# Two reorderings on ScalarE in a fused convolution, gate and projection kernel

## The chip, the cores and the metric

The kernel runs on one core of one Trainium2 chip. The metric is the device time of one execution in microseconds (us); lower is better. Three runs of the kernel before gave 386.8 to 387.71, with a median of 387.55.

A core has five engines with a queue each: TensorE (PE; its weight loads are shown as PEld), VectorE (DVE), ScalarE (ACT), GpSimd (POOL) and SyncE (SP, which only issues DMAs here). Each takes its instructions in the order of its own queue, and they wait for one another by semaphores. TensorE writes into PSUM, which has eight banks of 512 fp32 values per partition; VectorE and ScalarE read them.

## What is computed

The input `x` is 8 sequences of 4224 tokens with 192 channels, in 8 heads of 24. First comes a causal convolution of 7 taps whose weights are a softmax per head:

```python
w = np.exp(weight - np.max(weight, axis=-1, keepdims=True))
w = w / (np.sum(w, axis=-1, keepdims=True) + 1e-09)
out = np.einsum('hk,bskhg->bshg', w, x_unf)     # x_unf: 7 shifted views of x
```

Its result, called x from here on, is gated and projected:

```python
for k in range(K):                              # K = 5, one weight per channel
    gate_pre += conv_w[k][None, None, :] * xp[:, k:k + S, :]
gate = 1.0 / (1.0 + np.exp(-gate_pre))
val = x @ w_val
return (gate * val @ w_out).astype(np.float32)
```

All of it is in fp32.

## The kernel before

The tokens of four sequences lie one behind the other in the free dimension, and two such rows are worked on at once. Channels are on the partitions. Two halves of 128 channels, one per row of tokens (chunks 0 and 1), make tile `x1`; the other 64 channels of both rows make chunk 2, tile `x2`. Tokens are cut into 14 groups, and these into 37 blocks (`STEPS`): two of 288 tokens, six of 432, twenty-seven of 482, one of 500 and one of 244. A block is a step of the main loop.

The softmax convolution is done by TensorE as products with a banded matrix (`conv_unit`, L303). A unit is up to seven windows, each of four small matmuls (L319); it fills two PSUM banks named `pc`, which ScalarE copies to `e` (two copies, L330). Then SP (for the first groups also other queues) scatters finished heads from `e` into `x1` and `x2` of the group (L359) and loads further input (L165). Units run about two groups ahead of the blocks that use them: `todo[n]` (L548 to L553) says how many follow block n. For blocks 0 to 3 it is 2, 4, 2 and 3, for block 4 it is 3, for blocks 5 to 29 it is 2, for 30 and 31 it is 1, and then 0.

For a block n:

- The gate is accumulated in PSUM, in `pa` for chunks 0 and 1 and in `pb` for chunk 2, each with a single buffer. `gate_open` (L393, ScalarE) writes the first tap, `gate_taps` (L400, VectorE) adds the four others, and `gate_close` (L413, ScalarE) applies the sigmoid and writes `g1` or `g2`.
- `split` makes two parts of x for fast products: ScalarE casts (`xh`, L421 and L429), POOL subtracts (`xl`, L422 and L430).
- The first product, v = x times w_val, is built in three banks v0, v1, v2 by `diagonal` (L454), `main` (L464), `columns` (L492) and `rows` (L477), three matmuls or sixteen small ones each.
- `gated` (L511, VectorE) multiplies v by the gate in place, in the order chunk 2, 0, 1. `split_gated2` and `split_gated1` cast the results (`ph`, ScalarE, L429 and L421) and subtract on POOL (`pl`).
- The second product, o = gated values times w_out, runs one block later, by the same four functions, into banks o0, o1, o2. `project` copies a chunk to `ot` (ScalarE, L527); with the copy of chunk 1, the last, one DMA stores all three chunks (L532). For the last block there is a DMA for each chunk.

The order on every engine is written by hand: instructions enter each queue in the order of the program. The banks v, o and `pc` come from one pool, `ps`, with five buffers that go round in program order; a matmul that starts a new bank waits until the bank that held this buffer before has been read. In a step with two units the order of banks is v2, o2, v0, v1, o0, o1 and four for the units.

Blocks 0 to 3 have a loop of their own (L579), with a cruder order; there `now` says how many units go ahead of the gate of the next block. The other blocks, and one round more to end the last, are in the loop at L640. In it `main("o", n - 1, q)` and `project(n - 1, q)` belong to the block before, and `split_gated1(n)` to the present one.

Of the kernel before, what the change touches and what calls it, by code (L numbers as in the profile page):

```python
# [105 lines left out]
def kernel(  # L106
# [28 lines left out]
    o = 0  # L135
# [248 lines left out]
    def gate_open(n, i):  # L384
        if n >= N:
            return
        m = STEPS[n][2]
        if i == 0:
            acc = ps_g.tile([128, 2, 512], F32, tag="pa", name=f"pa_{n}")[:, :, :m]
        else:  # L390
            acc = ps_h.tile([128, 512], F32, tag="pb", name=f"pb_{n}")[:, :m]
        accs[n, i] = acc
        nc.scalar.mul(acc, views(n, 0)[i], cwt[:, i, 0:1])  # L393

    def gate_taps(n, i, k0=1, k1=KG):
        if n >= N:
            return
        acc = accs[n, i]
        for k in range(k0, k1):
            nc.vector.scalar_tensor_tensor(  # L400
                out=acc, in0=views(n, k)[i], scalar=cwt[:, i, k : k + 1],
                in1=acc, op0=ALU.mult, op1=ALU.add,
            )

    def gate_close(n, i):
        if n >= N:
            return
        m = STEPS[n][2]
        if i == 0:
            dst = g1s[n] = gp.tile([128, 2, MB], F32, tag="g1", name=f"g1_{n}")[:, :, :m]  # L410
        else:
            dst = g2s[n] = gp.tile([128, MB], F32, tag="g2", name=f"g2_{n}")[:, :m]
        nc.scalar.activation(dst, accs.pop((n, i)), AF.Sigmoid)  # L413
# [3 lines left out]
    def split1(pool, tag, n, x):  # L417
        m = STEPS[n][2]
        h = pool.tile([128, 2, MB], F32R, tag="h", name=f"{tag}h_{n}")[:, :, :m]
        l = pool.tile([128, 2, MB], F32R, tag="l", name=f"{tag}l_{n}")[:, :, :m]  # L420
        nc.scalar.copy(h, x)  # L421
        nc.gpsimd.tensor_tensor(out=l, in0=x, in1=h.bitcast(F32), op=ALU.subtract)  # L422
        return h, l
# [9 lines left out]
    def bank(what, n, q):  # L433
        t = ps.tile([128, 512], F32, tag="p", name=f"{what}_{n}_{q}")[:, : STEPS[n][2]]
        banks[what, n, q] = t
        return t

    def operands(what, n):
        return (w_val, *xs[n, 1], *xs[n, 2]) if what == "v" else (w_out, *pr[n, 1], *pr[n, 2])

    def parts(w, h, l):
        return (w.h, h), (w.l, h), (w.h, l)

    def ok(n):
        return 0 <= n < N

    def diagonal(what, n):
        if not ok(n):
            return
        acc = bank(what, n, 2)  # L450
        w, _, _, h2, l2 = operands(what, n)
        r = slice(W22, W22 + 128)
        for i, (a, b) in enumerate(parts(w, h2, l2)):
            nc.tensor.matmul(acc, lhsT=a[:, r], rhs=b, start=(i == 0), stop=False)  # L454

    def main(what, n, q):
        if not ok(n):
            return
        fresh = (what, n, q) not in banks
        acc = bank(what, n, q) if fresh else banks[what, n, q]  # L460
        w, h, l, _, _ = operands(what, n)
        r = slice(W11, W11 + 128)
        for i, (a, b) in enumerate(parts(w, h, l)):
            nc.tensor.matmul(  # L464
                acc, lhsT=a[:, r], rhs=b[:, q], start=(fresh and i == 0), stop=(not fresh and i == 2)
            )

    def rows(what, n):
        if not ok(n):
            return  # L470
        fresh = (what, n, 0) not in banks
        two = [bank(what, n, q) if fresh else banks[what, n, q] for q in range(2)]
        w, _, _, h2, l2 = operands(what, n)
        r = slice(W21, W21 + 128)
        for i, (a, b) in enumerate(parts(w, h2, l2)):
            for acc, p in zip(two, HALVES):
                nc.tensor.matmul(  # L477
                    acc, lhsT=a[p, r], rhs=b[p], start=(fresh and i == 0), stop=(not fresh and i == 2)
                )

    def columns(what, n):
        if not ok(n):
            return
        m = STEPS[n][2]
        acc = banks[what, n, 2]
        w = w_val if what == "v" else w_out
        x = views(n)[0] if what == "v" else g1s[n]
        cuts = [m * i // 4 for i in range(5)]
        for i in range(4):
            c = slice(cuts[i], cuts[i + 1])  # L490
            for q, p in enumerate(HALVES):
                nc.tensor.matmul(  # L492
                    acc[p, c], lhsT=w.f[:, W12 : W12 + 64], rhs=x[:, q, c],
                    start=False, stop=(i == 3),
                )

    def split(n):
        if n >= N:
            return
        x1, x2 = views(n)  # L500
        if n < 2:
            xs[n, 2] = split2(sp, "x", n, x2)
        xs[n, 1] = split1(sp, "x", n, x1)
        if n >= 2:
            xs[n, 2] = split2(sp, "x", n, x2)

    def gated(n, q):
        if not ok(n):
            return
        v = g1s[n][:, q] if q < 2 else g2s[n]  # L510
        nc.vector.tensor_tensor(out=v, in0=banks.pop(("v", n, q)), in1=v, op=ALU.mult)  # L511

    def split_gated1(n):
        if ok(n):
            pr[n, 1] = split1(pp, "p", n, g1s[n])

    def split_gated2(n):
        if ok(n):
            pr[n, 2] = split2(pp, "p", n, g2s[n])

    def project(n, q):
        if not ok(n):
            return
        m = STEPS[n][2]
        if n not in ots:
            ots[n] = op.tile([128, 3 * MB], F32, tag="ot", name=f"ot_{n}")
        nc.scalar.copy(ots[n][:, q * m : (q + 1) * m], banks.pop(("o", n, q)))  # L527
        o = 3 * sum(s[2] for s in STEPS[:n])
        if n == LAST:
            nc.sync.dma_start(out[:, o + q * m : o + (q + 1) * m], ots[n][:, q * m : (q + 1) * m])  # L530
        elif q == 1:
            nc.sync.dma_start(out[:, o : o + 3 * m], ots[n][:, : 3 * m])  # L532
# [9 lines left out]
    def conv(k):  # L542
        for _ in range(k):
            if done[0] < len(units):
                conv_unit(done[0])
                done[0] += 1

    todo = [0] * (N + 1)  # L548
# [30 lines left out]
    for n in range(HEAD):  # L579
        k = 2 if n < 2 else 3  # L580
        diagonal("v", n)
        split(n + 1)
        if n != 1:
            diagonal("o", n - 1)
        main("v", n, 0)
        main("v", n, 1)
        if n == 1:
            diagonal("o", n - 1)
        else:
            gate_taps(n + 1, 0, 1, k)  # L590
        columns("v", n)
        gated(n, 2)
        if n == 1:
            gate_taps(n + 1, 0, 1, k)
        columns("o", n - 1)
        split_gated2(n)
        project(n - 1, 2)
        rows("v", n)
        gated(n, 0)
        gated(n, 1)  # L600
        rows("o", n - 1)
        main("o", n - 1, 0)
        project(n - 1, 0)
        main("o", n - 1, 1)
        project(n - 1, 1)
        conv(1)
        split_gated1(n)
        now = todo[n] if n == 0 else todo[n] // 2
        conv(now - 1)
        gate_taps(n + 1, 0, k, KG)  # L610
        gate_close(n + 1, 0)
        gate_open(n + 2, 0)
        gate_taps(n + 1, 1)
        conv(todo[n] - now)
        gate_close(n + 1, 1)
        gate_open(n + 2, 1)
# [16 lines left out]
    def flush(i):  # L633
        for n, _ in [p for p in pending if p[1] == i]:
            gate_close(n, i)
            gate_open(n + 1, i)
            pending.remove((n, i))

    taps("AA")
    for n in range(HEAD, N + 1):  # L640
        diagonal("v", n)
        flush(1)
        split(n + 1)
        diagonal("o", n - 1)
        main("v", n, 0)
        main("v", n, 1)
        taps("AA")
        columns("v", n)
        gated(n, 2)
        flush(0)  # L650
        taps("B")
        columns("o", n - 1)
        split_gated2(n)
        project(n - 1, 2)
        rows("v", n)
        gated(n, 0)
        taps("B")
        gated(n, 1)
        rows("o", n - 1)
        split_gated1(n)  # L660
        main("o", n - 1, 0)
        taps("ABAB")
        project(n - 1, 0)
        main("o", n - 1, 1)
        project(n - 1, 1)
        conv(todo[n])
# [77 lines left out]
```

## Time and profile before

| | |
|---|---|
| median of three runs | 387.55 us (386.8 to 387.71) |
| the profiled execution | 383.81 us |
| its span, first to last instruction | 382.0 us |
| mean granted TensorE clock | 0.996 |
| HBM read and written over the span | 147 GB/s |

In the profile a row of a timeline is: start in us, duration in us, engine, line, operation, output <- inputs by the program's tile names, shape, and x with the number of instructions merged into the row. In brackets stands the idle time of the engine before the row, and after the arrow what ended it. A row of the waits is: who waited for whom: us in total, how many times, the longest. A row of the windows is: the window and its length in us, the busy time of PE, PEld, DVE, ACT and POOL in it with the number of instructions, the granted clock, the DMA share and GB/s. A matmul of plain fp32 data appears as two records. Ends of matmuls are modelled, and instructions of one engine may overlap by some tenths of a us, so the distance from one start to the next tells more of an engine's pace than a duration does.

### The profile page before, as it was taken

To read this page: it belongs to the slowest core of one execution; us is meant where nothing else is said; L and a number is where in the kernel's file an instruction comes from. 1 tells how busy PE (TensorE), PEld (TensorE's weight loads), DVE (VectorE), ACT (ScalarE), POOL (GpSimd) and SP (SyncE) were. 2 spreads that over 40 slices of the span, in tenths; PEclk is the share of its full clock that TensorE was granted. 3 is DMA by queue.
4 is the path that set the end of the run, shared out by engine and by line. 5 is a ranking of instruction groups with operands and counts; after the bars stand their busy time and mean duration, and the time that the engine had idled before them with its cause. 6 is when DMAs were issued, how large, how long until landed. Compare 5 with 4: busy or idle time off the path is not lost.

```text
span 382.0 us, 14551 instructions
## 1 busy us (share of the span) xinstructions
PE 356.5 (93%) x6130; PEld 289.1 (76%) x6130; DVE 331.7 (87%) x439; ACT 327.6 (86%) x570; POOL 251.1 (66%) x177
## 2 busy tenths in 40 slices
PE   8798988898999999999999999999999999999895
PEld 7776876787877777777777777777877777776684
DVE  3899889688998988999898898898898899999960
ACT  7589889879998898898898899899899999898863
POOL 1969655556666666666767766666667666677772
PEclk9899999999999999999999999999999999999999
DMA  8888787996986986986986996996898794431224
GB/s 272 232 250 252 223 284 224 257 266 202 277 266 171 258 273 189 238 264 196 243 262 187 205 270 205 232 288 204 203 272 252 177 297 143 140 114 78 79 104 174
DMA packets 38954, 83.30 MB, mean 218 GB/s; under 512 B 4936, under 2 KB 17008, under 8 KB 38888
## 3 DMA queue, kind: packets, MB, share of 16 engines
q1 hardware_dynamic: 37440, 80.64, 71.4%
q0 software_dynamic: 896, 1.27, 1.4%
q8 instruction: 48, 0.79, 0.9%
q10 hardware_dynamic: 552, 0.46, 0.4%
q14 instruction: 18, 0.15, 0.2%
HBM read 30.06 MB, written 26.00 MB: 147 GB/s over the span
## 4 chain that ended last, share of the span: by engine, by line
PE 43%; DVE 14%; ACT 13%; DMA 12%; POOL 9%; issue 5%; SPq 3%; DVEq 0%; ACTq 0%; POOLq 0%
DMA x<-e 11%; PE v L464 8%; DVE g L511 6%; PE pc L319 6%; ACT ph L421 6%; PE v L492 6%; PE v L477 5%; PE o L492 5%; DVE pb L400 5%; PE v L454 5%; PE o L454 4%; POOL pl L422 4%; ACT ot L527 3%; PE o L464 2%; SPq L359 2%
## 5 line engine op out<-in xcount | busy, mean ns | idle before, releaser
L400 DVE SCALAR_TENSOR_TENSOR pa<-x,cwt,pa 128x964 f32<-128x964 f32 (+4 forms) x148 | 173.2, 1170 | 2.3 <-ACT pa L393 0.4
L422 POOL TENSOR_TENSOR xl<-x,xh 128x964 fp32r<-128x964 f32 (+4 forms) x37 | 73.5, 1987 | 81.5 <-ACT xh L421 70.5
L400 DVE SCALAR_TENSOR_TENSOR pb<-x,cwt,pb 128x482 f32<-128x482 f32 (+4 forms) x148 | 102.4, 692 | 0.6
L422 POOL TENSOR_TENSOR pl<-g,ph 128x964 fp32r<-128x964 f32 (+4 forms) x37 | 79.6, 2152 | 29.1 <-ACT ph L421 25.1
L511 DVE TENSOR_TENSOR g<-v,g 128x482 f32<-128x482 f32 (+4 forms) x111 | 69.5, 631 | 32.8 <-PE v L492 20.0
L319 PE MATMUL pc<-band,x 64*56 64x58 f32 (+1 forms) x3776 | 74.4, 220 | 14.7 <-ACT ot L527 9.1
L319 PEld LDWEIGHTS pc<-band,x 64*56 64x56 f32 (+1 forms) x3776 | 65.3, 132 | 28.1 <-ACT ot L527 13.5
L330 ACT COPY e<-pc 120x348 f32<-120x348 f32 (+2 forms) x148 | 59.5, 489 | 5.1 <-PE pc L319 5.1
L527 ACT COPY ot<-o 128x482 f32<-128x482 f32 (+4 forms) x111 | 56.2, 538 | 3.0 <-PE o L464 2.4
L421 ACT CAST ph<-g 128x964 fp32r<-128x964 f32 (+4 forms) x37 | 35.4, 958 | 23.0 <-DVE g L511 22.8
L430 POOL TENSOR_TENSOR pl<-g,ph 128x482 fp32r<-128x482 f32 (+4 forms) x37 | 43.6, 1179 | 2.7 <-ACT ph L429 2.7
L430 POOL TENSOR_TENSOR xl<-x,xh 128x482 fp32r<-128x482 f32 (+4 forms) x37 | 42.0, 1136 | 3.2 <-ACT xh L429 3.1
L393 ACT ACTIVATE pa<-x,cwt 128x964 f32<-128x964 f32 (+4 forms) x37 | 38.1, 1030 | 2.8 <-DMA x<-e 1.7
L492 PEld LDWEIGHTS v<-x,wvf 128*64 128x64 f32 x592 | 29.3, 136 | 11.7 <-issue 10.8
L492 PE MATMUL v<-x,wvf 128*64 128x121 f32 (+5 forms) x592 | 37.4, 267 | 0.0
L492 PE MATMUL o<-g,wof 128*64 128x121 f32 (+5 forms) x592 | 35.5, 261 | 0.0
L413 ACT ACTIVATE g<-pa 128x964 f32<-128x964 f32 (+4 forms) x37 | 34.3, 927 | 1.2 <-DVE pa L400 1.1
L421 ACT CAST xh<-x 128x964 fp32r<-128x964 f32 (+4 forms) x37 | 34.8, 942 | 0.0
L464 PE MATMUL o<-ph,woh 128*128 128x482 f32 (+4 forms) x74 | 31.2, 421 | 0.0
L492 PEld LDWEIGHTS o<-g,wof 128*64 128x64 f32 x592 | 30.8, 136 | 0.1
L464 PE MATMUL v<-xh,wvh 128*128 128x482 f32 (+4 forms) x74 | 27.5, 372 | 1.2 <-ACT e L330 1.2
L464 PE MATMUL o<-pl,woh 128*128 128x482 f32 (+4 forms) x74 | 27.5, 372 | 0.0
(75 smaller groups left out, 568.8 us busy)
## 6 DMA issues: line engine op xcount, KB each, us to landing
x<-xw SPq DMA_DIRECT2D x72, 300.0 KB
out<-ot SPq DMA_DIRECT2D x27, 723.0 KB
x<-e SPq DMA_DIRECT2D x45, 271.9 KB
x<-xw SPq DMA_DIRECT2D x16, 360.0 KB
x<-e SPq DMA_DIRECT2D x36, 135.9 KB
out<-ot SPq DMA_DIRECT2D x6, 648.0 KB
x<-e SPq DMA_DIRECT2D x20, 163.1 KB
x<-e SPq DMA_DIRECT2D x18, 90.6 KB
```

What stands on the lines that cost most here:

```text
L319: nc.tensor.matmul(pc[r][c0:c1, k * HW : (k + 1) * HW], lhsT=xtiles[i][p, c + c0 : c + c1], rhs=band[p, 4 * q + hi, :], start=True, stop=True,
L330: nc.scalar.copy(ev[:, a : a + w, r, :], pc[r][:M, : w * HW].rearrange("p (w t) -> p w t", t=HW))
L393: nc.scalar.mul(acc, views(n, 0)[i], cwt[:, i, 0:1])
L400: nc.vector.scalar_tensor_tensor(out=acc, in0=views(n, k)[i], scalar=cwt[:, i, k : k + 1], in1=acc, op0=ALU.mult, op1=ALU.add,)
L421: nc.scalar.copy(h, x)
L422: nc.gpsimd.tensor_tensor(out=l, in0=x, in1=h.bitcast(F32), op=ALU.subtract)
L430: nc.gpsimd.tensor_tensor(out=l, in0=x, in1=h.bitcast(F32), op=ALU.subtract)
L454: nc.tensor.matmul(acc, lhsT=a[:, r], rhs=b, start=(i == 0), stop=False)
L464: nc.tensor.matmul(acc, lhsT=a[:, r], rhs=b[:, q], start=(fresh and i == 0), stop=(not fresh and i == 2))
L492: nc.tensor.matmul(acc[p, c], lhsT=w.f[:, W12 : W12 + 64], rhs=x[:, q, c], start=False, stop=(i == 3),)
L511: nc.vector.tensor_tensor(out=v, in0=banks.pop(("v", n, q)), in1=v, op=ALU.mult)
L527: nc.scalar.copy(ots[n][:, q * m : (q + 1) * m], banks.pop(("o", n, q)))
```

## The change

In the main loop (blocks 4 on) the product and the copy of the first output chunk move ahead of the cast of the gated values of chunks 0 and 1. In the loop of the first blocks `now` is rounded up instead of down; it is the number of units that go ahead of the gate.

```diff
@@ -605,7 +605,7 @@
         project(n - 1, 1)
         conv(1)
         split_gated1(n)
-        now = todo[n] if n == 0 else todo[n] // 2
+        now = todo[n] if n == 0 else (todo[n] + 1) // 2
         conv(now - 1)
         gate_taps(n + 1, 0, k, KG)
         gate_close(n + 1, 0)
@@ -657,10 +657,10 @@
         taps("B")
         gated(n, 1)
         rows("o", n - 1)
+        main("o", n - 1, 0)
+        project(n - 1, 0)
         split_gated1(n)
-        main("o", n - 1, 0)
         taps("ABAB")
-        project(n - 1, 0)
         main("o", n - 1, 1)
         project(n - 1, 1)
         conv(todo[n])
```

Since each engine has its own queue, a line that moves past lines of other engines moves nothing: `main` is TensorE's, `project` and the cast in `split_gated1` are ScalarE's, the subtraction in it is POOL's, `taps` is VectorE's.

## The prediction

> **What bounds the kernel now.** I read the page first, then the waits, the busy times of the long middle, and the timelines of each engine through a few steps.
>
> ```profile
> PE 356.5 (93%) x6130; PEld 289.1 (76%) x6130; DVE 331.7 (87%) x439; ACT 327.6 (86%) x570; POOL 251.1 (66%) x177
> ```
>
> ```profile
> PEld pc L319 <- ACT ot L527: 13.5, 29, 1.2
> PE pc L319 <- ACT ot L527: 9.1, 28, 0.9
> ```
>
> Four engines are nearly full, so shares decide nothing. The waits say more: TensorE, the busiest, stops 28 or 29 times at the convolution (L319) for ScalarE's copy of an output chunk (L527). In 25 steps (5 to 29) two convolution units follow the projections, so this is about one stop in each. One such step, TensorE first:
>
> ```profile
> 165.05 0.38 PE L464 MATMUL o<-pl,woh 128*128 128x482 f32 x1
> ...
> 166.02 1.14 PE L319 MATMUL pc<-band,x 64*64 64x58 f32 x58
> 167.42 1.03 PE L319 MATMUL pc<-band,x 64*56 64x58 f32 x54 [0.27 <-ACT ot L527]
> 168.39 0.49 PE L454 MATMUL v<-xh,wvh 128*128 128x482 f32 x1
> ```
>
> A unit of seven windows is 56 records (28 fp32 matmuls, two records each). The first convolution row holds 58: unit one and the first matmul of unit two. Then TensorE waits. The five banks of pool `ps` go round in program order: v2, o2, v0, v1, o0, o1, then two for each unit. So unit two takes the banks of v1 (free when VectorE has gated chunk 1) and of o0 (free when ScalarE has copied the first output chunk). Its first matmul writes the one, its second the other. ScalarE and VectorE at the same time:
>
> ```profile
> 164.59 0.55 ACT L527 COPY ot<-o 128x482 f32<-128x482 f32 x1
> 165.91 1.00 ACT L421 CAST ph<-g 128x964 fp32r<-128x964 f32 x1 [0.77 <-DVE g L511]
> 166.81 1.02 ACT L527 COPY ot<-o 128x482 f32<-128x482 f32 x2
> 167.72 1.71 ACT L330 COPY e<-pc 120x406 f32<-120x406 f32 x4
> 169.43 0.57 ACT L413 ACTIVATE g<-pb 128x482 f32<-128x482 f32 x1
> ```
>
> ```profile
> 165.23 0.65 DVE L511 TENSOR_TENSOR g<-v,g 128x482 f32<-128x482 f32 x1
> ...
> 168.68 0.72 DVE L400 SCALAR_TENSOR_TENSOR pb<-x,cwt,pb 128x482 f32<-128x482 f32 x1
> ...
> 172.41 0.66 DVE L511 TENSOR_TENSOR g<-v,g 128x482 f32<-128x482 f32 x1 [0.62 <-PE v L492]
> ```
>
> The chain reads: gating of chunk 1 ends at 165.88, the cast runs, then the copy of o0 (half of the pair at 166.81, done near 167.33), and at 167.42 TensorE goes on. Yet o0 was complete at 165.43 (165.05 + 0.38), and ScalarE idled 0.77 us just then, since the cast ahead of the copy waited for VectorE.
>
> **Part 1: the copy of o0 ahead of the cast.** In steps 4 to 36 two ScalarE instructions change places. No other queue is reordered: TensorE still gets both chunks of o in the same order, the subtraction on POOL follows the cast, and the one output DMA of a block hangs on the last copy, which keeps its place. Nothing is added or removed.
>
> The copy can start when o0 is complete, about 165.5. A copy holds ScalarE for 0.46 (half of 167.72 - 166.81, two copies from start to next start), so the cast may start at 165.96 instead of 165.91: the copy fits into the idle 0.77 and delays the cast by 0.05. Unit two's bank is then free near 166.1, long before unit one ends. TensorE gains the time from the first unit to the next diagonal, less that of unstalled units. A lone unit of six windows gives the rate, and the next step the case of 6+7:
>
> ```profile
> 325.80 0.92 PE L319 MATMUL pc<-band,x 64*64 64x58 f32 x48
> 326.65 0.49 PE L454 MATMUL v<-xh,wvh 128*128 128x482 f32 x1
> ```
>
> ```profile
> 176.03 1.02 PE L319 MATMUL pc<-band,x 64*64 64x58 f32 x50
> 177.45 1.03 PE L319 MATMUL pc<-band,x 64*56 64x58 f32 x54 [0.40 <-ACT ot L527]
> 178.41 0.48 PE L454 MATMUL v<-xh,wvh 128*128 128x482 f32 x1
> ```
>
> Six windows take 0.85 (326.65 - 325.80), so seven take 0.99. Units of 7+7 take 2.37 now (168.39 - 166.02) and 1.98 unstalled: 0.39 saved. 6+7 take 2.38 against 1.84: 0.54. The third step of a group, 7+6, I count like 7+7, as its first unit is as long. A group of three steps saves 1.32, a mean step 0.44. Steps 8 to 29 are 22 steps: 22 x 0.44 = 9.7 us. As a check, the wait row above has 13.5/29 = 0.47 a stop.
>
> What is late next, with a step shortened from 10.02 (168.39 to 178.41) to about 9.6? The next diagonal needs o1's bank: cast done near 166.95, copy of o1 near 167.45, and unit two now ends at 168.0, so 0.5 to spare. For the other engines, the busy times of 22 steps:
>
> ```profile
> 100.00:320.00 220.00, 212.91 (x3703) 170.99 (x3703) 199.09 (x243) 199.00 (x332) 146.34 (x88) 1.00 0.82 234
> ```
>
> VectorE and ScalarE (third and fourth number) have 9.05 of work a step (199/22). Both stay under 9.6. VectorE waits 0.62 for TensorE ahead of gating chunk 2 and keeps about 0.2 of it. ScalarE waits for VectorE's last tap before it closes pb (tap ends at 169.40, close starts at 169.43), so there too VectorE's pace and not its own decides. TensorE becomes the bound, without a stop.
>
> A stop of this shape is named in the Trainium skill: "Perfetto Trace Analysis", section Identifying Performance Opportunities, says that the same gap repeating on the engine that should be saturated can mean that there isn't enough PSUM for the next tile. By that alone a new order would only move the gap to the next bank, and nothing would be won. The spare 0.5 us at o1's bank speaks against it here.
>
> For steps 4 to 7 I count 0.5 us, one step's worth: the stop is there too, but ScalarE waits in step 6 for a transfer, which a faster TensorE doesn't bring:
>
> ```profile
> 85.32 1.07 ACT L393 ACTIVATE pa<-x,cwt 128x964 f32<-128x964 f32 x1 [1.68 <-DMA x<-e]
> ```
>
> From step 30 on one unit or none is left, and VectorE bounds: it works without idle, 8.86 us a step. The cast comes 0.46 later there, off that path. I take nothing.
>
> ```profile
> 334.43 1.22 DVE L400 SCALAR_TENSOR_TENSOR pa<-x,cwt,pa 128x964 f32<-128x964 f32 x1
> ...
> 343.29 1.22 DVE L400 SCALAR_TENSOR_TENSOR pa<-x,cwt,pa 128x964 f32<-128x964 f32 x1
> ```
>
> **Part 2: block 3.** Steps 0 to 3 have 2, 4, 2 and 3 units; only step 3 is odd, so `now` changes there alone, from 1 to 2. Again only ScalarE's queue is reordered: the two copies of that step's second unit go ahead of closing and opening pa. The unit's loads and scatters keep their order on SP; they may issue about 1.9 us sooner (copies from 56.19 instead of 58.05).
>
> ```profile
> 56.19 0.91 ACT L413 ACTIVATE g<-pa 128x864 f32<-128x864 f32 x1
> 57.12 0.98 ACT L393 ACTIVATE pa<-x,cwt 128x864 f32<-128x864 f32 x1
> 58.05 1.58 ACT L330 COPY e<-pc 120x406 f32<-120x406 f32 x4
> ```
>
> ```profile
> 58.14 4.60 DVE L400 SCALAR_TENSOR_TENSOR pa<-x,cwt,pa 128x864 f32<-128x864 f32 x4 [0.42 <-ACT pa L393]
> ...
> 73.90 0.61 DVE L511 TENSOR_TENSOR g<-v,g 128x432 f32<-128x432 f32 x1 [3.09 <-PE v L492]
> ```
>
> ```profile
> 58.59 0.46 PE L454 MATMUL o<-ph,woh 128*128 128x432 f32 x1 [1.74 <-ACT e L330]
> ...
> 70.10 0.21 PE L319 MATMUL pc<-band,x 64*64 64x58 f32 x1 [1.50 <-issue]
> ```
>
> Two of the four copies take 0.79 (half of 1.58), so pa opens 0.79 later and VectorE's taps start at 58.93 instead of 58.14. TensorE's stop of 1.74, for the second unit's bank, ends sooner. Bounds: 1.74 gained, if TensorE led; 0.79 lost, if VectorE does. VectorE is nearer, as it has no pause behind 58.14 for some ten us. But its delay meets 1.50 idle of TensorE at 70.10, 3.09 of its own at 73.90 and ScalarE's 1.68 at 85.32, each of which can swallow it. So I take 0; without that cover it costs the 0.79.
>
> **Sum.** 9.7 + 0.5 + 0 = 10.2 us. The profiled execution took 383.81 us, with a span of 382.0, which should become about 371.8. The median of the runs shown lies 3.7 above the profiled execution, which nothing in the profile explains; I carry the saving over in us: 387.55 - 10.2 = 377.3.
>
> **Rivals.**
> *Transfers take part of it.* The row of the long middle has a DMA share of 0.82, and between two groups of three steps the engines drain for about one slice:
>
> ```profile
> 146.00:148.00 2.00, 1.61 (x86) 1.40 (x88) 2.00 (x3) 2.00 (x4) 1.07 (x2) 1.00 0.04 11
> ```
>
> That is 1.9 us (2.00 x 0.96) a group, of which the change takes 1.32. If uneven queues need more, pa is opened late, as at 85.32, and about half of the gain goes: 387.55 - 5 = 382.5. For it: 0.6 us left is little. Against: opening pa has waited for a transfer once in the whole run.
>
> *The copy holds up the cast.* This is the slower case. Were o0 complete only after chunk 1 is gated, the cast would stand behind the copy. ScalarE has 0.97 to spare a step (10.02 - 9.05), so it decides from o0 complete some 0.45 + 0.97 - 0.46 = 0.96 later than now (near 166.4 in that step); each further 0.1 costs 25 x 0.1 = 2.5 us, hence 390 at 0.1 beyond. Against: TensorE's order is unchanged, and o0 is complete 0.45 ahead of the gating. The Trainium skill has the rule behind this in "TensorE: Matmul & The Clock Gate", section Architectural detail: ScalarE's queue is a strict FIFO. The trace agrees, as the cast's wait of 0.77 holds up the copies now.
>
> *The gap moves to the next bank.* If the copy of o1 came as late as unit two's end plus the old stop, the time would stay at 387.5. Against: the 0.5 to spare, above.
>
> **How the numbers follow.** Chances: forecast 0.70 (own range 375 to 380), transfers 0.18, gap moves 0.08, copy holds up the cast 0.04. The low end, 375.0, is all 13.5 us of the wait row less 29 x 0.03 for what unstalled units still take. The high end, 384.0, reaches past the transfers' case. A run can tell about 0.3%, 1.2 us, from no change: faster 0.88, same 0.08, slower 0.04.
>
> **What would show it.** In the changed profile the convolution's wait for L527 should be all but gone; each middle step should have one copy, the cast, one copy on ScalarE, the first copy starting while VectorE gates; units should follow each other without a gap; from step to step it should be 9.5 to 9.65; VectorE's wait for L492 should fall from 0.6 to about 0.2. In step 3 the taps should start 0.8 later, and the end of step 6 should not. New waits of pa's opening (L393) for x<-e, of the cast for the copy, or of the diagonal (L454) for L527 would prove me wrong.

## The result, and the profile after

| | before | after | predicted |
|---|---|---|---|
| median, runs side by side | 387.18 us (383.8 to 387.71, 4 runs) | 372.6 us (371.32 to 372.8, 4 runs) | 377.3 (375.0 to 384.0) |
| ratio, 95% interval | | 0.9634 (0.9574 to 0.9694) | 0.9736 |
| span of the profiled execution | 382.0 us | 370.9 us | 371.8 us |

The change is faster, as forecast, but by 14.6 us where 10.2 were expected, and the time lies below the range. Medians here and below are of all runs, while the ratios leave out those that took over 1.5% longer than the fastest of their kernel. The profile of after, first its busy shares, then TensorE's weight loads in the list of waits, then the long middle in the view by windows:

```profile
PE 348.1 (94%) x6130; PEld 283.8 (77%) x6130; DVE 330.2 (89%) x439; ACT 325.1 (88%) x570; POOL 251.1 (68%) x177
```

```profile
PEld pc L319 <- ACT ot L527: 5.7, 17, 0.5
```

```profile
100.00:320.00 220.00, 218.67 (x3856) 177.12 (x3854) 209.53 (x257) 207.79 (x350) 155.02 (x93) 1.00 0.82 245
```

The shares hardly moved (TensorE 93 to 94%), although the span is 2.9% shorter. The stop for ScalarE's copy fell from 13.5 us in 29 pieces to 5.7 in 17, and what is left overlaps with matmuls that still run: in 220 us of the middle TensorE is idle for 1.3, before for 7.1; and the 1.3 are two single stops near 300 and 307 us (0.41 and 0.92), of which the last section tells. One middle step of after on TensorE, ScalarE and VectorE (timelines):

```profile
210.24 1.74 PE L319 MATMUL pc<-band,x 64*64 64x58 f32 x104
211.91 0.48 PE L454 MATMUL v<-xh,wvh 128*128 128x482 f32 x1
...
219.56 1.86 PE L319 MATMUL pc<-band,x 64*64 64x58 f32 x112
221.35 0.49 PE L454 MATMUL v<-xh,wvh 128*128 128x482 f32 x1
```

```profile
209.44 1.02 ACT L527 COPY ot<-o 128x482 f32<-128x482 f32 x2
210.35 1.01 ACT L421 CAST ph<-g 128x964 fp32r<-128x964 f32 x1
211.24 0.57 ACT L527 COPY ot<-o 128x482 f32<-128x482 f32 x1
211.70 1.62 ACT L330 COPY e<-pc 120x406 f32<-120x406 f32 x4
213.66 0.58 ACT L413 ACTIVATE g<-pb 128x482 f32<-128x482 f32 x1 [0.34 <-DVE pb L400]
```

```profile
208.25 0.66 DVE L511 TENSOR_TENSOR g<-v,g 128x482 f32<-128x482 f32 x1 [0.34 <-PE v L477]
208.83 0.72 DVE L400 SCALAR_TENSOR_TENSOR pb<-x,cwt,pb 128x482 f32<-128x482 f32 x1
209.45 0.66 DVE L511 TENSOR_TENSOR g<-v,g 128x482 f32<-128x482 f32 x1
```

Both units of a step are now one row of 104 or 112 records without a gap (13 or 14 windows). On ScalarE the copies of o2 and o0 stand together ahead of the cast (the pair at 209.44). VectorE's gating of chunk 1 (L511, the second of these rows) ends at 210.11; the cast starts at 210.35, as the pair makes way. From diagonal to diagonal it is 9.44 here (211.91 to 221.35), and before 10.02.

The starts of the diagonals of v in two profiles of each kernel split the time into stretches (us; "again" is a second profile, from the experiments):

| stretch | before | after | before again | after again | saved, first pair | saved, second pair | predicted |
|---|---|---|---|---|---|---|---|
| start to block 8 | 98.68 | 99.99 | 98.40 | 97.39 | -1.31 | 1.01 | 0.5 |
| block 8 to block 30 | 219.46 | 207.03 | 219.47 | 205.41 | 12.43 | 14.06 | 9.7 |
| block 30 to the end | 63.89 | 63.91 | 63.84 | 63.76 | -0.02 | 0.08 | 0 |
| span | 382.03 | 370.93 | 381.71 | 366.56 | 11.10 | 15.15 | 10.2 |

The middle is the same to 0.01 us in both profiles of before. (The second came as quick as the first, 383.58 us, so where slower executions of before lose their time was not seen.) After has 205.41 there, or 207.03 with single stops near block 30 (the last section). The start differs by some us from execution to execution: after reaches block 8 at 99.99 or at 97.39. Its first profile came late in both stretches, so the two spans, 11.1 apart, understate what the runs show.

### The profile page after: what moved, and what is told of

The parts are those of the page before. It is cut to its first block, busy times and chain, and to the rows that moved or that the text cites. A ratio compares the mean times of both kernels' runs of the same rounds, so it can differ in the third digit from the quotient of the medians.

```text
span 370.9 us, 14551 instructions
## 1 busy us (share of the span) xinstructions
PE 348.1 (94%) x6130; PEld 283.8 (77%) x6130; DVE 330.2 (89%) x439; ACT 325.1 (88%) x570; POOL 251.1 (68%) x177
## 4 chain that ended last, share of the span: by engine, by line
PE 70%; ACT 8%; DMA 6%; DVE 6%; POOL 5%; issue 4%; SPq 1%; ACTq 0%; DVEq 0%; POOLq 0%
PE pc L319 12%; PE o L464 11%; PE v L464 10%; PE v L492 8%; PE o L492 7%; PE v L477 7%; PE v L454 6%; PE o L454 5%; PE o L477 5%; DVE pa L400 3%; DMA x<-e 3%; DMA x<-xw 3%; DVE pb L400 2%; ACT g L413 2%; POOL xl L422 2%
## 5 line engine op out<-in xcount | busy, mean ns | idle before, releaser
L511 DVE TENSOR_TENSOR g<-v,g 128x482 f32<-128x482 f32 (+4 forms) x111 | 69.6, 631 | 21.9 <-PE v L477 12.1
L319 PE MATMUL pc<-band,x 64*64 64x58 f32 (+1 forms) x3776 | 66.7, 218 | 10.7 <-DMA x<-xw 5.3
L319 PEld LDWEIGHTS pc<-band,x 64*56 64x56 f32 (+1 forms) x3776 | 60.4, 130 | 20.4 <-ACT ot L527 5.7
L527 ACT COPY ot<-o 128x482 f32<-128x482 f32 (+4 forms) x111 | 57.2, 541 | 7.6 <-PE o L464 7.5
L330 ACT COPY e<-pc 120x348 f32<-120x348 f32 (+2 forms) x148 | 59.5, 495 | 3.9 <-PE pc L319 3.9
L492 PEld LDWEIGHTS v<-x,wvf 128*64 128x64 f32 x592 | 29.5, 138 | 11.8 <-issue 10.0
L492 PE MATMUL v<-x,wvf 128*64 128x121 f32 (+5 forms) x592 | 37.7, 269 | 0.0
L492 PE MATMUL o<-g,wof 128*64 128x121 f32 (+5 forms) x592 | 35.8, 261 | 0.4 <-issue 0.4
L413 ACT ACTIVATE g<-pb 128x482 f32<-128x482 f32 (+4 forms) x37 | 20.6, 556 | 14.9 <-DVE pb L400 14.8
L492 PEld LDWEIGHTS o<-g,wof 128*64 128x64 f32 x592 | 30.9, 136 | 0.8 <-issue 0.6
L464 PE MATMUL o<-ph,woh 128*128 128x482 f32 (+4 forms) x74 | 31.2, 421 | 0.0
L464 PE MATMUL v<-xh,wvh 128*128 128x482 f32 (+4 forms) x74 | 27.9, 377 | 2.4 <-ACT e L330 2.4
```

The lines of the kernel that those rows point to most:

```text
L319: nc.tensor.matmul(pc[r][c0:c1, k * HW : (k + 1) * HW], lhsT=xtiles[i][p, c + c0 : c + c1], rhs=band[p, 4 * q + hi, :], start=True, stop=True,
L330: nc.scalar.copy(ev[:, a : a + w, r, :], pc[r][:M, : w * HW].rearrange("p (w t) -> p w t", t=HW))
L464: nc.tensor.matmul(acc, lhsT=a[:, r], rhs=b[:, q], start=(fresh and i == 0), stop=(not fresh and i == 2))
L492: nc.tensor.matmul(acc[p, c], lhsT=w.f[:, W12 : W12 + 64], rhs=x[:, q, c], start=False, stop=(i == 3),)
```

## The experiments

### Each part alone, both again, and neither

The theory: the whole gain is part 1's, from the bank of o0; part 2 is hidden or costs up to 0.8. Rivals: part 2 gains too, or the gain depends on both. For part 1 alone, only the second hunk of the diff is applied; for part 2 alone only the first.

> Main loop reordered, block 3 as before. Theory (the gain is all in the bank of o0): steps 8 to 29 take 9.36 us each instead of 9.99, so 13 to 14 us less than the kernel before, and 0.8 us less than the whole change, since the taps of step 5 aren't opened late. Rival (the two parts need each other): less than 10 us gained.

> Block 3 alone changed, main loop as before. Theory: the taps in step 3's end start 0.8 us later, and later idle time swallows between nothing and all of it: 0 to 0.8 us slower than the kernel before. Rival (earlier banks help TensorE): up to 1.7 us faster.

> The whole change again, for the same chip as the two parts. Theory: the sum of the two, 13 to 14.6 us faster than the kernel before; steps of 9.3 to 9.45 us.

> The kernel before, unchanged, profiled once more. Theory (the first profiled execution, 383.8 us, was a quick one): the loss of some 3 us against it stands in the first steps, up to step 5, and steps 8 to 29 keep 9.99 us. Rival (steps of the middle differ from one execution to the next): the steps of the middle are longer than 9.99 us.

| | median | ratio, 95% interval | block 8 to block 30 |
|---|---|---|---|
| part 1 alone | 368.68 us | 0.9595 (0.9548 to 0.9642) | 207.10, with one stop of 1.43 and its wake |
| part 2 alone | 385.14 us | 1.0015 (0.9982 to 1.0048) | 220.62, with one stop near block 30 |
| both again | 371.81 us | 0.9651 (0.9599 to 0.9702) | 205.41 |
| before | 384.63 us | 1 | 219.47 |

Part 1 has the whole gain. Its undisturbed middle steps are those of both parts (median 9.33 us, before 10.01). What part 2 does can't be read from the medians, whose intervals overlap, but it can from block 3. ScalarE and VectorE there, with part 1 alone (so block 3 as before):

```profile
56.38 0.93 ACT L421 CAST ph<-g 128x864 fp32r<-128x864 f32 x1
57.19 0.91 ACT L413 ACTIVATE g<-pa 128x864 f32<-128x864 f32 x1
58.13 0.98 ACT L393 ACTIVATE pa<-x,cwt 128x864 f32<-128x864 f32 x1
```

```profile
59.15 4.60 DVE L400 SCALAR_TENSOR_TENSOR pa<-x,cwt,pa 128x864 f32<-128x864 f32 x4 [0.42 <-ACT pa L393]
```

and with part 2 alone:

```profile
56.31 0.92 ACT L421 CAST ph<-g 128x864 fp32r<-128x864 f32 x1
57.12 0.91 ACT L330 COPY e<-pc 120x406 f32<-120x406 f32 x2
57.90 0.93 ACT L413 ACTIVATE g<-pa 128x864 f32<-128x864 f32 x1
58.86 0.99 ACT L393 ACTIVATE pa<-x,cwt 128x864 f32<-128x864 f32 x1
```

```profile
59.88 4.60 DVE L400 SCALAR_TENSOR_TENSOR pa<-x,cwt,pa 128x864 f32<-128x864 f32 x4 [1.23 <-ACT pa L393]
```

From the cast to the taps it is 2.77 us without part 2 and 3.57 with it: the two copies that went ahead, 0.80. Is that swallowed later? Between block 3's and block 5's diagonals lies TensorE's stop for no shown reason ("issue"), whose length changes from execution to execution. Taken away, what is left is steady:

| | diagonal 3 to 5 | stop "issue" | the rest |
|---|---|---|---|
| before | 25.17 | 1.50 | 23.67 |
| before again | 24.47 | 0.77 | 23.70 |
| part 1 alone | 25.84 | 2.16 | 23.68 |
| part 2 alone | 26.71 | 2.22 | 24.49 |
| after | 26.77 | 2.27 | 24.50 |
| both again | 25.51 | 1.02 | 24.49 |

Part 2 costs 0.80 us, and nothing swallows it. In both again a second such stop (1.11, ended at 57.25) falls into the stretch and the rest is still 24.49: this pause of TensorE cost nothing there, and the later opening of pa its full length, so VectorE leads. The best version by the profiles is therefore part 1 alone.

### Which bank decides

The theory says that unit two waits for the bank of o0, and that it helps only because this bank is now copied ahead of the cast. Then giving unit two the bank of o1, which is still copied behind the cast, must bring the stop back with ScalarE's order unchanged. The rival: the earlier copy helps by itself, as it fills idle time of ScalarE. A first try asked for the tiles of o1 and o0 in the other order, on top of part 1:

```diff
-        two = [bank(what, n, q) if fresh else banks[what, n, q] for q in range(2)]
+        if fresh:
+            for q in (1, 0) if what == "o" else (0, 1):
+                bank(what, n, q)
+        two = [banks[what, n, q] for q in range(2)]
```

> Part 1 alone, with the banks of the second product taken in the order o1, o0, so that unit two waits for the copy of o1, which still comes behind the cast; ScalarE's order is that of part 1. Theory (what counts is that unit two's bank is copied early): TensorE stops again by about 0.55 us a step, steps of about 9.95, 12 us slower than part 1 alone, near 381. Rival (what counts is that ScalarE no longer idles ahead of the cast): like part 1 alone, steps of 9.36.

It took 369.97 us, ratio 0.9622 (0.9582 to 0.9661), with middle steps of 9.33. This tells nothing: in the program that came out, unit two's second bank was still that of o0, since the pool gave every tile the same bank as without the swap. So the pool of five was replaced by five pools of one buffer, taken in turn; once with the tiles of o in the usual order, and once with the swap above.

```diff
-    ps = ctx.enter_context(tc.tile_pool(name="ps", bufs=5, space=PSUM))
+    five = [ctx.enter_context(tc.tile_pool(name=f"ps{i}", bufs=1, space=PSUM)) for i in range(5)]
+    asked = [0]
+    class ps:
+        @staticmethod
+        def tile(shape, dtype, tag, name):
+            asked[0] += 1
+            return five[asked[0] % 5].tile(shape, dtype, tag=tag, name=name)
```

> The product and copy of the first output chunk stay ahead of the cast; block 3 as before. The five shared PSUM banks now go round strictly, each in a pool of its own. Theory (unit two's second bank is o0's, as it was): middle steps of 9.36 us and 369 to 372 us, like part 1 alone. Rival (the way in which banks are given out matters by itself): steps longer than 9.45.

> As the strict rotation, but the second output chunk takes its bank first, so that unit two's second bank is now that of o1, which is still copied behind the cast. ScalarE's order is that of part 1. Theory (the bank decides): TensorE stops again at the convolution for L527, 0.5 to 0.65 us a step; middle steps of 9.9 to 10.0, 383 to 386 us, all of the gain gone. Rival (the earlier copy gains by itself, through ScalarE's idle time or its order): steps of 9.36 and 369 to 372 us.

| | median | ratio, 95% interval | median middle step |
|---|---|---|---|
| turns, usual order | 370.05 us | 0.9657 (0.9596 to 0.9718) | 9.33 us |
| turns, o1 takes its bank first | 384.51 us | 1.0021 (0.9986 to 1.0055) | 10.02 us |

The swap takes back the whole gain. In it the lines are shifted: L327 is the convolution, L538 the copy of an output chunk, L472 the product, L429 the cast. Its list of waits, and one step on TensorE and on ScalarE:

```profile
PEld pc L327 <- ACT ot L538: 14.3, 31, 0.7
```

```profile
207.77 1.02 PE L327 MATMUL pc<-band,x 64*64 64x58 f32 x50
209.19 1.03 PE L327 MATMUL pc<-band,x 64*56 64x58 f32 x54 [0.41 <-ACT ot L538]
210.15 0.49 PE L462 MATMUL v<-xh,wvh 128*128 128x482 f32 x1
```

```profile
207.22 0.56 ACT L538 COPY ot<-o 128x482 f32<-128x482 f32 x1 [0.43 <-PE o L472]
207.68 1.00 ACT L429 CAST ph<-g 128x964 fp32r<-128x964 f32 x1
208.57 0.56 ACT L538 COPY ot<-o 128x482 f32<-128x482 f32 x1
```

TensorE stops again after 50 records (unit one and the first matmul of unit two) until the copy behind the cast is done near 209.1, and this at the same ScalarE order that was fast. Order on ScalarE is worth nothing by itself; it counts by the bank that it frees.

### Both output copies ahead of the cast

Part 1, and the product and copy of the second chunk ahead of the cast too, which tests the rival in which the cast is held up:

```diff
         main("o", n - 1, 0)
         project(n - 1, 0)
-        split_gated1(n)
-        taps("ABAB")
         main("o", n - 1, 1)
         project(n - 1, 1)
+        split_gated1(n)
+        taps("ABAB")
```

> Part 1 with both product chunks and both copies ahead of the cast. Theory (TensorE leads and ScalarE has room): the cast starts 0.45 us later, the units' copies as before, steps of 9.36, the same time as part 1 alone within 1 us. Rival (whatever holds up the cast is paid for): 0.45 us a step more, 11 us slower than part 1 alone.

371.42 us, ratio 0.9633 (0.9604 to 0.9662), median middle step 9.33. One step on ScalarE and on TensorE:

```profile
211.38 1.47 ACT L527 COPY ot<-o 128x482 f32<-128x482 f32 x3
212.74 1.01 ACT L421 CAST ph<-g 128x964 fp32r<-128x964 f32 x1
```

```profile
212.18 1.74 PE L319 MATMUL pc<-band,x 64*64 64x58 f32 x104
213.84 0.48 PE L454 MATMUL v<-xh,wvh 128*128 128x482 f32 x1
```

The cast starts 1.10 ahead of the diagonal, in after 1.56 (210.35 to 211.91): 0.46 later, one copy, and the step is no longer. So in the middle a cast that is late by one copy costs nothing.

### What a unit costs by itself

The step that failed in the prediction was the time of unstalled units, taken as 0.99 for seven windows and 0.85 for six, each with its own share of what lies around a unit. In after two units in a row take 1.67 or 1.79. Is the missing part a price of the change between the small matmuls of the convolution and the wide ones? On top of part 1, the product of the second output chunk was put between the two units, so that there are two changes more in a step, and nothing else to compute:

```diff
         taps("ABAB")
+        conv(todo[n] - 1)
         main("o", n - 1, 1)
         project(n - 1, 1)
-        conv(todo[n])
+        conv(min(todo[n], 1))
```

> Part 1, but in the main loop the two units of a step no longer follow each other: the product of the second output chunk stands between them, with its copy. Theory (a run of units costs 0.12 us a window and one fixed part where TensorE changes from the small matmuls to the wide ones, about 0.1 at each change): two changes more, so middle steps of 9.5 to 9.7 instead of 9.36, 373 to 377 us. Rival (each unit carries its own fixed part, 0.85 and 0.99 as the prediction took it, wherever it stands): steps stay at 9.36, 369 to 372 us.

It took 378.92 us, ratio 0.9883 (0.9838 to 0.9927), with a median middle step of 9.75: 0.42 above part 1. Both the time and the step lie a little above what was expected (373 to 377 us, 9.5 to 9.7). One step on TensorE:

```profile
222.36 0.39 PE L464 MATMUL o<-pl,woh 128*128 128x482 f32 x1
222.68 1.04 PE L319 MATMUL pc<-band,x 64*64 64x58 f32 x56
223.65 0.48 PE L464 MATMUL o<-ph,woh 128*128 128x482 f32 x1
223.97 0.37 PE L464 MATMUL o<-ph,wol 128*128 128x482 f32 x1
224.18 0.38 PE L464 MATMUL o<-pl,woh 128*128 128x482 f32 x1
224.49 1.05 PE L319 MATMUL pc<-band,x 64*64 64x58 f32 x56
225.48 0.48 PE L454 MATMUL v<-xh,wvh 128*128 128x482 f32 x1
```

Apart, two units of seven windows take 0.97 and 0.99, which is the prediction's figure; together they take 1.79. The wide matmuls beside them pay as well: 0.31 or 0.32 to the next start, where one wide matmul follows another at 0.21 or 0.22 (223.97 to 224.18). Two changes more are 1.96 - 1.79 = 0.17 in the units and 2 x 0.10 at the wide matmuls, 0.37 together; this step has 9.82 (215.66 to 225.48), and 9.44 in after. (The diagonal needs the bank of o1, whose copy is done only near 225.5 here, so up to 0.02 of the 0.99 may be that wait.) The windows of this kernel show no idle time for it:

```profile
100.00:320.00 220.00, 219.96 (x3758) 172.29 (x3757) 203.34 (x249) 205.80 (x339) 149.59 (x91) 1.00 0.77 236
```

TensorE counts as busy for 219.96 of 220 us, more than in after, and gets through fewer records. That such a price needs neither small matmuls nor plain fp32 data, only a change of tile, can be seen in after, where `rows` (L477, 64*128) is followed by `main` (L464, 128*128), both of fast products:

```profile
208.20 0.38 PE L477 MATMUL o<-ph,wol 64*128 64x482 f32 x2
208.42 0.38 PE L477 MATMUL o<-pl,woh 64*128 64x482 f32 x2
208.72 0.48 PE L464 MATMUL o<-ph,woh 128*128 128x482 f32 x1
209.05 0.38 PE L464 MATMUL o<-ph,wol 128*128 128x482 f32 x1
209.26 0.38 PE L464 MATMUL o<-pl,woh 128*128 128x482 f32 x1
```

From start to start it is 0.22 within `rows`, 0.30 at the change, 0.33 behind it and then 0.21 again.

### No unit ahead of the gate in block 3

If two units ahead of the gate cost 0.80 against one, does none gain another 0.8? On top of part 1:

```diff
-        conv(1)
+        now = todo[n] if n == 0 else todo[n] // 2 if n < 3 else 0
+        conv(min(now, 1))
         split_gated1(n)
-        now = todo[n] if n == 0 else todo[n] // 2
         conv(now - 1)
```

> Part 1, and in block 3 no unit ahead of the gate: the opposite of part 2. Theory (VectorE leads there, and pa's opening is what it waits for): the taps of step 5 start 0.4 us sooner, 12.7 us after step 3's first diagonal matmul instead of 13.1, and about 0.4 us of time. Rival (TensorE leads, for want of banks): up to 1.6 us slower than part 1 alone.

371.33 us, ratio 0.965 (0.9619 to 0.9682). The taps start 12.58 after block 3's diagonal instead of 13.09, so 0.51 sooner, but block 3 to block 5 takes 25.76 with a stop "issue" of 1.33: 24.43 are left, 0.75 more than with one unit ahead. TensorE now waits there for the banks of the units, one stop being this:

```profile
59.45 1.43 PE L319 MATMUL pc<-band,x 64*56 64x58 f32 x46 [1.99 <-ACT e L330]
```

One unit ahead, as before the change, is the best of the three.

### The stops without a shown reason

The last experiment puts 32 small matmuls, whose results aren't used, at the start of part 1's kernel, to see whether TensorE's single stops "issue" stay with a place in the code or with a number of instructions:

```diff
     zeros(WARM[0])
+    pw = ps.tile([128, 512], F32, tag="p", name="pw")
+    for i in range(32):
+        nc.tensor.matmul(pw[:M, :8], lhsT=zero[:, :M], rhs=zero[:, M : M + 8], start=True, stop=True)
```

> Part 1 with 32 small matmuls more at the start (64 more matmul records and as many weight loads; they write a bank that nobody reads). Theory (TensorE's stops without a releaser are late transfers of its own instructions, 16 KB or some 127.5 matmul records at a time): a stop again lies at the matmul record number 1362 of the execution or a multiple of 127.5 away from it, so 64 records earlier in the program. Rival (they belong to the last matmul of block 4's third unit): a stop at record 1426, which is that same matmul.

380.79 us, ratio 0.9882 (0.9842 to 0.9922). The time says little, since the added matmuls took 10.4 us at the start, ahead of the first unit. The stops in the middle were these two:

```profile
92.62 0.78 PE L495 MATMUL v<-x,wvf 128*64 128x108 f32 x12 [1.24 <-issue]
...
156.01 0.45 PE L322 MATMUL pc<-band,x 64*56 64x58 f32 x14 [0.83 <-issue]
```

They are taken up in the last section.

## Why the prediction was right in its mechanism and wrong in its size

**The bound and its cause: right.** TensorE stopped for the bank of o0, held behind a cast that itself waited. That it was this bank is shown by the two kernels that take the banks in turn: which bank unit two gets is worth 14.5 us (370.05 against 384.51).

**ScalarE's side of part 1: right.** The copy lies in the idle time, the cast starts as soon as the pair of copies is done, 0.24 behind the gating (210.11 to 210.35). That this little delay costs nothing is shown by the kernel with both copies ahead. The row of waits for L527 isn't all but gone, as the prediction had it: 5.7 us of the weight loads' waits stay, but no stop of TensorE in the middle.

**The saving per step: the mechanism was right, the size was wrong, and this is the step that failed.** The prediction set unstalled units at 1.98 (7+7) and 1.84 (6+7 and 7+6 by length) from a lone unit of six windows. In after they take 1.79 (219.56 to 221.35) and 1.67 (210.24 to 211.91):

| units | stopped, before | unstalled, taken | unstalled, measured | saved, taken | saved, measured |
|---|---|---|---|---|---|
| 7+7 | 2.37 | 1.98 | 1.79 | 0.39 | 0.58 |
| 6+7 | 2.38 | 1.84 | 1.67 | 0.54 | 0.71 |
| 7+6 | 2.25 | counted like 7+7 | 1.67 | 0.39 | 0.58 |

A lone unit holds the passage to the wide matmuls as well, about 0.13 (0.85 less six windows at 0.12). Scaling it to seven windows and taking it twice counts this part more than twice; two units in a row pay it once. The prediction's own rows had the rate: 58 records in 1.14 and 50 in 1.02 are one window more for 0.12, so 14 windows and one passage are 14 x 0.12 + 0.13 = 1.81, and 13 are 1.69. That saves 0.56 (7+7 and 7+6) and 0.69 (6+7), 0.6 in the mean, and 22 x 0.6 = 13 in the middle. The units as measured give 0.62 in the mean and 13.7, of the 14.06 by which the middle is shorter. The Trainium skill names what such a passage is: "TensorEngine Tiling (Array Packing)", section Key Properties, says that changing the tiling mode drains TensorE. It gives no price; the kernel with the units apart agrees, with 0.42 us a step for two changes more, though no view shows a drain as such.

**The comparison with the waits failed with it.** 13.5/29 = 0.47 a stop looked like support for 0.44, and the low end of the range took those 13.5 us as a ceiling. By the profiles part 1 is worth 14.06 from block 8 to 30 and 1.34 from block 5 to 8 (27.60 in before again, 26.26 in both again), 15.4 in all. A row of waits counts the time in which the weight load waited, not what a stop costs TensorE.

**What is late next: right.** TensorE became the bound, with 1.3 idle of 220. VectorE and ScalarE are at 209.53 and 207.79 in the same window, so about 8.9 and 8.8 of a step of 9.34. In the middle VectorE's wait in the gating of chunk 2 (0.62 for L492 before) is gone, where 0.2 was expected to stay, and that for L477 stays at 0.34. With 9.34 a step the time between the end of o1's copy (211.24 + 0.57 = 211.81) and the diagonal that needs its bank (211.91) is 0.1, not the 0.5 taken; it still holds.

**Blocks 4 to 7: undersized.** 0.5 was taken, with the wait for a transfer at 85.32 as the reason. This wait was an accident of the one profile: before again has 9.22 for that step, not 10.06, and of the other profiles only that of the padded kernel has such a wait there (3.20, at 96.25). So 1.3 us are gained, all of them in blocks 5 to 7; block 4 gains nothing (23.70 in before again and 23.68 with part 1 alone, from block 3 to 5).

**From block 30 on: right**, nothing (63.84 and 63.76).

**Part 2: wrong.** It was taken as hidden in idle times of fixed place. They have none: TensorE's stop, whatever its length (1.50 there, 0.62 to 2.27 in the others), moves along with the work ahead of it (it begins 24.36 us after block 3's diagonal in after, 23.53 in before), and the waits behind it follow. The bound that the prediction gave for this case, 0.79 lost, is what was measured (0.80).

**From the profile to the runs: right, within the spread of the runs.** The saving was carried over in us to a median above the profiled execution. The terms as measured in the profiles, 14.06 in the middle, 1.34 ahead of it and 0.80 lost in block 3, make 14.6, and the medians lie 14.58 apart. That this agrees so closely is luck: beside each other in the experiments the medians of before and both again lie 12.8 apart (384.63 and 371.81).

**The rivals.** Transfers took no part in the middle: the DMA share stays at 0.82, the rate rises from 234 to 245 GB/s, and the steps are even. The gap didn't move to the next bank, though that was nearer (0.1) than thought. The rule of the Trainium skill beside this rival, that a repeating gap can mean too little PSUM ("Perfetto Trace Analysis", section Identifying Performance Opportunities), agrees with the kernel that takes o1's bank first, where the gap is back, and not with the change, where the same five banks do. The cast wasn't held up.

## What to carry to other kernels

Where one engine's queue frees buffers in PSUM for another, put the copy that frees the bank needed first ahead of work that itself waits, and trace by name which bank the next writer gets: the same order was worth 14.5 us with one bank and nothing with another. Take the price of unstalled work from how its time grows between two sizes (here 0.12 a window), not from a lone piece with its passages, and don't use a row of waits as a ceiling for what a stop costs. Idle time behind a delayed instruction covers the delay only if it ends at a time that doesn't move with it.

## What the runs showed of the hardware

**Passages between small and wide matmuls.** A convolution row of 48 records takes 0.92, of 96 records 1.62, of 104 records 1.74 and of 112 records 1.86. The first wide matmul behind it holds the next one back by 0.32 instead of 0.22. The same stands between products with 64-row tiles and with full ones: 0.30 and 0.33 instead of 0.22. No view shows this as idle time.

**Instructions that come late.** In 11 of the 12 profiles of these kernels without padding TensorE stops at matmul record 1362 of the trace, for 0.62 to 2.27 us and for no reason that the profile shows; more such stops come and go at records 220, 472, 726, 1107, 4039, 5442 and 5569 (at the last the profile names a copy, L330). The distances are about multiples of 127.5 records (4039 - 1362 = 21 x 127.5). The queue of instructions, from the list of DMA queues of after, with packets, MB and the share of the engines' time:

```profile
q8 instruction: 48, 0.79, 0.9%
```

48 transfers of 16 KB for 6130 matmuls and 6130 weight loads are one for some 255 instructions, or 127.5 pairs. In each of the 33 such stops of 0.4 us or more, in all 13 profiles, a transfer of this queue ended 1.2 to 1.6 us ahead of the stop's end (72.18 before 73.61 in after), while from one transfer to the next it is some 7 us. In the padded kernel, with 64 records more in front, the stops are at records 1617 and 2765, which are 2 and 11 x 127.5 behind 1362, and none is at 1426, where the code of the old stop had gone. So it is the number that counts and not the place, and the likeliest cause is a block of instructions that arrives late; why some come late and others not was not settled. The Trainium skill, "Runtime: NRT & Kernel Launch", section Instruction fetch mechanics, has the blocks of 16 KB and says that their cost is mostly hidden. Most are here, too: of 48, one to five are seen as a stop of 0.4 us or more. But one can last 2.3 us. Such stops, and a start that varies by some us, probably make much of the spread between runs (368.35 to 372.39 for both again) that hides what part 2 costs; the runs without a profile can't show it.
